# Paced loads, DMA transposes from block 10, and masks, inverse RMS and sink keys given to GpSimd, in an attention and SwGLU kernel

## The chip, the cores and the metric

One core of a Trainium2 chip. The metric is the device time of one execution, in microseconds. The kernel before takes 254.73 us (median of 3 runs, 254.19 to 254.93). A kernel that is only looked at gets a few runs; one that is compared closely gets 3 or 5 rounds next to the kernel before on the same chip.

Engines, as the profile abbreviates them: PE is TensorE (matmuls), PEld its weight loads, DVE VectorE, ACT ScalarE, POOL GpSimd, SP SyncE (here it only issues DMAs).

## The reference, cut to what matters

Attention with 4 sink keys and a window of 128, over 4 sequences of 768 tokens with 8 heads of 64, followed by RMSNorm and a SwGLU layer (512 to 1536 to 512):

```python
keep   = is_sink | in_window
scores = np.where(keep, q @ k.T / sqrt(D), -1e9)
a      = softmax(scores);  x = a @ v                     # (3072, 512)

rms  = np.sqrt(np.mean(x * x, axis=-1, keepdims=True) + 1e-06)
xn   = x / rms * rms_g
g    = xn @ w_gate
silu = g * (1.0 / (1.0 + np.exp(-g)))
out  = (silu * (xn @ w_val)) @ w_out
```

## The kernel before

Tokens go through in 24 blocks of 128, six to a sequence. For each block: load q, k, v; transpose q and k; scores, exp, mask; `a @ v` in two halves (`pv`), each normalised on VectorE to `x`; square and row sum on ScalarE (`sq`, `ms`); inverse square root in six operations of 128 x 1 (`m`, then five `y`); the scaled row `xr`; its transpose `xnt`. Four blocks make one group for the SwGLU layer: `pg` and `pvl` are the gate and value matmuls, `th` the tanh on ScalarE, `p` and `hT` two VectorE operations, `po` the matmuls with `w_out`. TensorE's program order is fixed by hand: attention of later blocks is woven into the SwGLU matmuls of an earlier group. What the change and the argument touch (`...` marks cuts):

```python
DMA_T_FROM = 12; POOL_MASK_FROM = 2
MANUAL = {PE, SP}                       # engines whose order is fixed by hand (names shortened)
ld = ctx.enter_context(tc.tile_pool(name="ld", bufs=3 * NT))   # 18 buffers for each of q and k
...
with tc.issue_after(last_load):         # everything from block 8 on, queued at once
    for g in range(2 * GB, NB):
        load_q(g); load_k(g); load_v(g)             # DMAs issued by GpSimd
...
def by_dma(g):
    return g >= DMA_T_FROM and g % NT > 0           # not the first block of a sequence
def unit_t(g):
    ...
    if by_dma(g):
        for i, src in enumerate((QS.pop(g), KS_.pop(g))):
            nc.sync.dma_start_transpose(out=QKT[b][:, i, :, t * P:(t + 1) * P], ...)
        return
    ps = ...; transposes(ps, ...); transposes(ps, ...); nc.scalar.copy(...)   # PE, then ACT
def unit_sink(b):
    ks = sink.tile([P, HP * KSW], BF16, name="ksk")
    nc.vector.memset(ks, 0.0)
    ... 2 x nc.vector.tensor_copy(out=ksv[...], in_=QKT[b][pr, 1, :, 0:NS])
def mask(ev, b, t, nq):
    if b < POOL_MASK_FROM or t == 0:
        nc.vector.tensor_tensor(out=e, in0=e, in1=mv, op=ALU.mult); return
    nc.gpsimd.affine_select(...)                    # one, or two of 128x512
...
def unit_av(g, u):
    ...                                             # pv matmuls
    unit_norm(g, u, pvv)                            # DVE: rden, x
    unit_sq(g, u)                                   # ACT: sq, ms
    if u == 1: unit_rms(g)                          # DVE: m, five y, then xr
def unit_rms(g):
    nc.vector.scalar_tensor_tensor(out=m, in0=ms[:, 0:1], scalar=RMS_EPS, in1=ms[:, 1:2], ...)
    nc.vector.tensor_scalar(out=y[:, 0:1].bitcast(I32), in0=m.bitcast(I32), ...)
    ... four more nc.vector.scalar_tensor_tensor, 128 x 1
    unit_xr(g)
def unit_xr(g):
    nc.vector.scalar_tensor_tensor(out=XR[g][-1], in0=x16[:, c], scalar=y[:, 4:5], in1=gb[:, c], ...)
```

The softmax here doesn't subtract the row's maximum and nothing guards it: scores larger than these inputs give would overflow.

## Time and profile before

| | before |
|---|---|
| median of 3 runs | 254.73 us |
| profiled span | 252.6 us |
| PE busy | 238.8 us (95%), so 13.8 us idle |
| granted PE clock | full throughout |
| DVE busy, POOL busy | 181.1 us, 98.1 us |

The page of the kernel before: the span, each engine's busy time with its share and its count of instructions, then rows of 40 slices of 6.3 us. A digit is the busy share of a slice in tenths; in the row PEclk it is the granted clock.

```profile
span 252.6 us, 4804 instructions
PE 238.8 (95%) x1733; PEld 127.4 (50%) x1760; DVE 181.1 (72%) x474; ACT 139.6 (55%) x312; POOL 98.1 (39%) x129
...
PE   5988979989999999999999999999999999999994
...
DVE  5666869889779999539989459988359991287700
...
POOL 8996779289985763134041004044201000000000
PEclk9999999999999999999999999999999999999999
```

From the tenth slice on the PE row is all nines up to the tail: a kernel that TensorE bounds. VectorE is also at nine in many slices and yet does not stop TensorE. (A row of nines means 90% or more; the clock here is full.)

### The profile page before, as it was taken

To read this page: it belongs to the slowest core of one execution; us is meant where nothing else is said; L and a number is where in the kernel's file an instruction comes from. 1 tells how busy PE (TensorE), PEld (TensorE's weight loads), DVE (VectorE), ACT (ScalarE), POOL (GpSimd) and SP (SyncE) were. 2 spreads that over 40 slices of the span, in tenths; PEclk is the share of its full clock that TensorE was granted. 3 is DMA by queue.
4 is the path that set the end of the run, shared out by engine and by line. 5 is a ranking of instruction groups with operands and counts; after the bars stand their busy time and mean duration, and the time that the engine had idled before them with its cause. 6 is when DMAs were issued, how large, how long until landed. Compare 5 with 4: busy or idle time off the path is not lost.

```text
span 252.6 us, 4804 instructions
## 1 busy us (share of the span) xinstructions
PE 238.8 (95%) x1733; PEld 127.4 (50%) x1760; DVE 181.1 (72%) x474; ACT 139.6 (55%) x312; POOL 98.1 (39%) x129
## 2 busy tenths in 40 slices
PE   5988979989999999999999999999999999999994
PEld 1446858655555454454454454454454544444441
DVE  5666869889779999539989459988359991287700
ACT  2757858879886465556473546466545441323211
POOL 8996779289985763134041004044201000000000
PEclk9999999999999999999999999999999999999999
DMA  9999999999999999650120550321321013200022
GB/s 130 152 174 189 189 156 188 182 155 150 194 186 161 155 131 155 128 168 13 21 56 10 145 145 3 64 58 19 113 84 23 0 21 98 91 0 0 0 86 83
DMA packets 105850, 25.74 MB, mean 102 GB/s; under 512 B 95074, under 2 KB 102754, under 8 KB 105827
## 3 DMA queue, kind: packets, MB, share of 16 engines
q0 software_dynamic: 80704, 13.90, 76.5%
q1 hardware_dynamic: 24082, 11.28, 18.6%
q10 hardware_dynamic: 1040, 0.26, 0.5%
q8 instruction: 14, 0.23, 0.4%
q14 instruction: 10, 0.07, 0.1%
HBM read 28.31 MB, written 6.29 MB: 137 GB/s over the span
## 4 chain that ended last, share of the span: by engine, by line
PE 67%; DMA 12%; DVE 8%; POOL 7%; ACT 2%; issue 2%; POOLq 0%; ACTq 0%; DVEq 0%
PE po L622 23%; PE pvl L581 18%; PE pg L581 18%; DMA wv<-in_moe_w_val_dram 7%; DMA ks<-in_k_dram 5%; PE pT L413 3%; DVE p L599 2%; POOL v L124 2%; POOL qs L111 2%; DVE hT L607 2%; PE pv L456 1%; PE pv L452 1%; PE pv L444 1%; POOL ks L111 1%; ACT et L422 1%
## 5 line engine op out<-in xcount | busy, mean ns | idle before, releaser
L581 PE MATMUL pg<-xnt,wg 128*128 128x512 bf16 (+1 forms) x317 | 73.5, 352 | 1.1 <-ACT xnt L567 0.5
L581 PE MATMUL pvl<-xnt,wv 128*128 128x512 bf16 (+1 forms) x322 | 73.4, 353 | 0.4
L622 PE MATMUL po<-wo,hT 128*128 128x512 bf16 x279 | 64.9, 379 | 0.5 <-issue 0.2
L594 ACT ACTIVATE th<-pg 128x512 bf16<-128x512 f32 x72 | 42.9, 596 | 39.1 <-PE pg L581 39.0
L599 DVE SCALAR_TENSOR_TENSOR p<-th,pg 128x512 bf16<-128x512 bf16 x72 | 48.9, 679 | 20.1 <-ACT th L594 19.5
L607 DVE TENSOR_TENSOR hT<-p,pvl 128x512 bf16<-128x512 bf16 x72 | 49.2, 684 | 3.7 <-PE pg L581 0.5
L581 PEld LDWEIGHTS <-wv 128*128 128x128 bf16 x328 | 30.5, 98 | 27.2 <-issue 1.1
L581 PEld LDWEIGHTS <-wg 128*128 128x128 bf16 x328 | 30.4, 98 | 26.9 <-issue 1.2
L422 ACT ACTIVATE et<-pT 128x512 bf16<-128x512 f32 x76 | 39.8, 602 | 4.8 <-PE pT L413 4.6
L390 POOL TENSOR_SCALAR_AFFINE_SELECT et<-et 128x512 bf16<-128x512 bf16 x20 | 13.1, 660 | 73.9 <-ACT et L422 73.9
L622 PEld LDWEIGHTS <-hT 128*128 128x128 bf16 x288 | 26.7, 98 | 29.7 <-issue 0.8
L494 ACT ACTIVATE sq<-x 128x256 bf16<-128x256 bf16 x48 | 20.0, 417 | 26.5 <-DVE x L484 26.1
L629 ACT ACTIVATE osb<-po 128x512 f32<-128x512 f32 x24 | 14.4, 602 | 25.9 <-PE po L622 20.8
L111 POOL DMA_DIRECT2D qs<-in_q_dram x23 | 20.7, 900 | 7.9 <-DMA wo<-in_moe_w_out_dram 2.2
L124 POOL DMA_DIRECT2D v<-in_v_dram x24 | 21.7, 903 | 4.4 <-DMA qs<-in_q_dram 2.6
L111 POOL DMA_DIRECT2D ks<-in_k_dram x23 | 20.6, 895 | 6.4 <-DMA wo<-in_moe_w_out_dram 3.2
L484 DVE TENSOR_TENSOR x<-pv,rden 128x256 bf16<-128x256 f32 x48 | 20.2, 421 | 0.8
L541 DVE SCALAR_TENSOR_TENSOR xr<-x,y,gb 128x512 bf16<-128x512 bf16 (+1 forms) x25 | 19.8, 795 | 0.7
L479 DVE RECIPROCAL rden<-pv 128x4 f32<-128x4 f32 x48 | 8.4, 175 | 16.1 <-PE pv L456 16.0
L388 DVE TENSOR_TENSOR et<-et,masks 128x1024 bf16<-128x1024 bf16 (+1 forms) x22 | 13.9, 638 | 3.5 <-ACT et L422 3.5
L456 PE MATMUL pv<-v,et 128*128 128x65 bf16 x168 | 15.3, 193 | 0.0
L452 PE MATMUL pv<-v,et 128*128 128x65 bf16 x136 | 12.7, 193 | 0.0
(75 smaller groups left out, 213.1 us busy)
## 6 DMA issues: line engine op xcount, KB each, us to landing
out_dram<-osb SPq DMA_DIRECT2D x24, 256.0 KB, 2.2
v<-in_v_dram POOLq DMA_DIRECT2D x24, 128.0 KB, 7.9
qs<-in_q_dram POOLq DMA_DIRECT2D x23, 128.0 KB, 8.2
ks<-in_k_dram POOLq DMA_DIRECT2D x23, 128.0 KB, 7.7
wg<-in_moe_w_gate_dram POOLq DMA_DIRECT2D x6, 256.0 KB, 7.6
wv<-in_moe_w_val_dram POOLq DMA_DIRECT2D x6, 256.0 KB, 8.2
wo<-in_moe_w_out_dram POOLq DMA_DIRECT2D x2, 768.0 KB, 10.6
osb<-in_k_dram ACTq DMA_DIRECT2D x1, 256.0 KB, 4.8
```

What stands on the lines that cost most here:

```text
L111: nc.gpsimd.dma_start(out=tl, in_=src[b, :, t * P:(t + 1) * P, :].rearrange("h t d -> t h d"),)
L124: nc.gpsimd.dma_start(out=V16[b][:, t, :, 0:D], in_=v[b, :, t * P:(t + 1) * P, :].rearrange("h t d -> t h d"),)
L422: nc.scalar.activation(out=et[:, hi].rearrange("p j n c -> p (j n c)"), in_=banks[u][hi], func=ACT.Exp, scale=inv_sqrt_d,)
L456: nc.tensor.matmul(out=dest, lhsT=E[(g, h, 0)], rhs=V16[b][:, t, h, :], start=(t == 0), stop=True, skip_group_check=True,)
L484: nc.vector.tensor_tensor(out=X16[g][:, heads_of(g, u), :], in0=pvv[:, :, 0:D], in1=RDEN.pop((g, u)).unsqueeze(2).to_broadcast((P, 4, D)), ...
L494: nc.scalar.activation(out=sq, in_=xh, func=ACT.Square, scale=MS_SCALE, accum_out=MS[g][:, u:u + 1],)
L541: nc.vector.scalar_tensor_tensor(out=XR[g][-1], in0=x16[:, c], scalar=y[:, 4:5], in1=gb[:, c], op0=ALU.mult, op1=ALU.mult,)
L581: nc.tensor.matmul(out=ps[:, i * n:(i + 1) * n], lhsT=w_sb[:, kt, ft * P:(ft + 1) * P], rhs=XNT[G][:, kt, cols], start=(kt == 0), stop=(kt ...
L594: nc.scalar.activation(out=st["th"], in_=st["pg"], func=ACT.Tanh, scale=0.5)
L599: nc.vector.scalar_tensor_tensor(out=p1, in0=st["th"], scalar=1.0, in1=st["pg"], op0=ALU.add, op1=ALU.mult,)
L607: nc.vector.tensor_tensor(out=HT[key][:, i:i + n, cols], in0=p1.rearrange("p (n c) -> p n c", n=n), in1=pvl.rearrange("p (n c) -> p n c", ...
L622: nc.tensor.matmul(out=st["po"], lhsT=HT[(G, ft // 2)][:, ft % 2, tb * P:(tb + 1) * P], rhs=wo[:, ft, :], start=(ft == 0), stop=(ft == FTN ...
```

## The change

Its intent: take load off TensorE (blocks 10, 11, 12 and 18 transposed by DMA) and off VectorE (six tiny operations of each block from 6, the masks of sequence 1 and the sink keys of sequences 1 to 3 to GpSimd), and issue the loads six blocks ahead instead of all at once, so that GpSimd, whose order is now fixed by hand too, comes to its other work. The diff, cut to its core:

```diff
-    DMA_T_FROM = 12
+    DMA_T_FROM = 10
+    LD = 4
+    AHEAD = 6
-    POOL_MASK_FROM = 2
-    MANUAL = {mybir.EngineType.PE, mybir.EngineType.SP}
+    POOL_MASK_FROM = 1
+    POOL_RMS_FROM = 6
+    MANUAL = {mybir.EngineType.PE, mybir.EngineType.SP, mybir.EngineType.Pool}
-    ld = ctx.enter_context(tc.tile_pool(name="ld", bufs=3 * NT))
+    ld = ctx.enter_context(tc.tile_pool(name="ld", bufs=LD))
-    with tc.issue_after(last_load):
-        for g in range(2 * GB, NB):
-            load_q(g); load_k(g); load_v(g)
+    def unit_load(g):
+        load_q(g); load_k(g); load_v(g)
     def by_dma(g):
-        return g >= DMA_T_FROM and g % NT > 0
+        return g >= DMA_T_FROM
     def unit_sink(b):
-        nc.vector.memset(ks, 0.0)
+        eng = nc.vector if b == 0 else nc.gpsimd
+        eng.memset(ks, 0.0)                      # the two copies likewise
     def unit_rms(g):
+        eng = nc.vector if g < POOL_RMS_FROM else nc.gpsimd
+        def fma(out, a, s1, op, s2, op1=ALU.mult):
+            eng.tensor_scalar(out=out, in0=a, scalar1=s1, scalar2=s2, op0=op, op1=op1)
-        ... one tensor_scalar and five scalar_tensor_tensor on nc.vector
+        fma(m, ms[:, 0:1], RMS_EPS, ALU.add, ms[:, 1:2], ALU.add)
+        ... five more fma: the same sums, as tensor_scalar with two scalar operands
     # in step(g):
+        if g + AHEAD < NB:
+            slots[2].append(lambda: unit_load(g + AHEAD))
```

More of the change, by code (lines that the diff above doesn't have):

```diff
@@ L238 @@
         load_wo(0)
-        last_load = load_wo(1)
-    with tc.issue_after(last_load):
-        for g in range(2 * GB, NB):
-            load_q(g)
-            load_k(g)
-            load_v(g)
+        load_wo(1)
     QKT, KSK, VSK, ESK, E, X16, MS, XR, XNT = {}, {}, {}, {}, {}, {}, {}, {}, {}
@@ L267, in unit_t1 @@
         )
+    def unit_load(g):
+        load_q(g)
+        load_k(g)
+        load_v(g)
     def by_dma(g):
-        return g >= DMA_T_FROM and g % NT > 0
+        return g >= DMA_T_FROM
     def unit_t(g):
@@ L296, in unit_sink @@
             pr = slice(hi * D, (hi + 1) * D)
-            nc.vector.tensor_copy(
+            eng.tensor_copy(
                 out=ksv[pr, :, hi * NS:(hi + 1) * NS],
@@ L469, in unit_av @@
             unit_rms(g)
-    PV, RDEN = {}, {}
+    PV, RDEN, LAST = {}, {}, [None]
     def heads_of(g, u):
@@ L483, in unit_norm @@
             unit_recip(g, u, pvv)
-        nc.vector.tensor_tensor(
+        LAST[0] = nc.vector.tensor_tensor(
             out=X16[g][:, heads_of(g, u), :], in0=pvv[:, :, 0:D],
             in1=RDEN.pop((g, u)).unsqueeze(2).to_broadcast((P, 4, D)), op=ALU.mult,
-        )
+        ).ins
     def unit_sq(g, u):
@@ L502, in unit_rms @@
         m = small.tile([P, 1], FP32, name="m")
-        nc.vector.scalar_tensor_tensor(
-            out=m, in0=ms[:, 0:1], scalar=RMS_EPS, in1=ms[:, 1:2],
-            op0=ALU.add, op1=ALU.add,
-        )
         y = small.tile([P, 5], FP32, name="y")
-        nc.vector.tensor_scalar(
-            out=y[:, 0:1].bitcast(I32), in0=m.bitcast(I32), scalar1=-0.5,
-            scalar2=float(0x5f3759df - 2 ** 31), op0=ALU.mult, op1=ALU.add,
-        )
-        nc.vector.scalar_tensor_tensor(
-            out=y[:, 1:2], in0=y[:, 0:1], scalar=y[:, 0:1], in1=m,
-            op0=ALU.mult, op1=ALU.mult,
-        )
-        nc.vector.scalar_tensor_tensor(
-            out=y[:, 2:3], in0=y[:, 1:2], scalar=RSQRT_B, in1=y[:, 1:2],
-            op0=ALU.add, op1=ALU.mult,
-        )
-        nc.vector.scalar_tensor_tensor(
-            out=y[:, 3:4], in0=y[:, 1:2], scalar=RSQRT_A, in1=y[:, 0:1],
-            op0=ALU.subtract, op1=ALU.mult,
-        )
-        nc.vector.scalar_tensor_tensor(
-            out=y[:, 4:5], in0=y[:, 2:3], scalar=RSQRT_C, in1=y[:, 3:4],
-            op0=ALU.add, op1=ALU.mult,
-        )
+        def fma(out, a, s1, op, s2, op1=ALU.mult):
+            eng.tensor_scalar(out=out, in0=a, scalar1=s1, scalar2=s2, op0=op, op1=op1)
+        fma(m, ms[:, 0:1], RMS_EPS, ALU.add, ms[:, 1:2], ALU.add)
+        fma(y[:, 0:1].bitcast(I32), m.bitcast(I32), -0.5, ALU.mult,
+            float(0x5f3759df - 2 ** 31), ALU.add)
+        fma(y[:, 1:2], y[:, 0:1], y[:, 0:1], ALU.mult, m)
+        fma(y[:, 2:3], y[:, 1:2], RSQRT_B, ALU.add, y[:, 1:2])
+        fma(y[:, 3:4], y[:, 1:2], RSQRT_A, ALU.subtract, y[:, 0:1])
+        fma(y[:, 4:5], y[:, 2:3], RSQRT_C, ALU.add, y[:, 3:4])
         Y[g] = y
@@ L734 @@
         ], first=True)
-        slots = [[lambda: unit_t1(5, 0)], [lambda: unit_t1(5, 1)], [lambda: unit_s(4)], [lambda: unit_sink_scores(0, 4)], [lambda: unit_t(6)], []]
+        slots = [[lambda: unit_t1(5, 0)], [lambda: unit_t1(5, 1), lambda: unit_load(8)], [lambda: unit_s(4)], [lambda: unit_sink_scores(0, 4), lambda: unit_load(9)], [lambda: unit_t(6)], [lambda: unit_load(10)]]
         for g in range(5, NB + 3):
```

## The prediction

> **What bounds it now.** TensorE. The busy table gives PE 95%, and the matmuls also run at rate: four 128x512 matmuls take 0.86 us wherever they stand in a row (chain of waits). Counting the columns of all matmuls at that rate, about 236 of the 252.6 us are streaming. By ten-us stretches, the 60 to 249 us part is about full; the idle is at the start (3.2 us in 0-10), in loads (1.3, 1.0, 1.6 us in 10-40, 1.4 us in 50-60, of which 1.2 us waits for q and k of block 8 behind w_out), and 3.7 us of tail. DMA is 90% or more busy for the first 105 us, but after 60 us PE no longer waits for it. DVE is 94-98% busy in several stretches (80-100, 150-170, 190-210) and stands in the chain there, yet PE hardly loses time.
>
> **What changes, costed.**
> 1. Blocks 10, 11, 12 and 18 are transposed by DMA: 4 x 0.44 us of PE (eight 128-column transposes) and 4 ACT copies of 1.01 us go. PE gain: 1.7 us, the only sure one.
> 2. DVE loses six tiny operations of each block from 6 (about 1.15 us a block, 20 us in all), the masks of blocks 7-11 (8 x 0.69 and 2 x 0.42 us) and most sink-key work. It was not what limited PE, so this buys little.
> 3. POOL gains this and must now run in program order: per block 3 load issues (0.88 us each = 2.6), masks 4 x 0.6 = 2.4, inverse RMS as six mostly dependent operations (estimate 0.26 us each, from two dependent 128x8 selects that started 0.26 us apart: 1.5 us). That is 6.5 us a block, while blocks 7-10 pass through PE in 5.3 to 6 us.
> 4. The loads from block 8 are paced. The first 50 us of DMA keep their order, so the wait for block 8 stays.
>
> **Where it hurts.** With four load buffers, POOL's load of block 12 waits for the DMA transposes of block 10, whose k lands near 57 us (issue 49.95 + 7.0). Transposes landed 7-8 us after issue under the full queue, 2.4 us when free; so that load is issued near 59-61, and behind it in order stand the masks of block 7 and the sink keys of sequence 1. PE wanted them at 60.9 and 60.4 (sink scores); I expect them near 64-66. POOL then has work without a break to about 85 us and lags again for the masks of block 8 and the inverse RMS of blocks 6 and 7, whose xr the PE transposes need. PE stalls of 5-7 us in 60-85. Later, DVE's fixed order holds xr right behind the norm, so it waits for square, then POOL: 1-2 us a block, giving back what it saved, with up to 1-3 us lost where the w_out matmuls wait for the last hT.
>
> The Trainium skill (GPSIMD Engine Reference, Key points) says POOL shares SBUF interfaces with VectorE; this trace agrees: one y operation took 0.60 us at 154.6 beside POOL's mask and 0.15 us at 164.6 without.
>
> **Sum.** 254.7 - 1.7 + about 7 = 260 us. Range 254 to 267. Faster by 2% would need 5 us, more than the removed PE work can give.
>
> **What would show it.** PE streaming down 1.7 us; PE idle in 60-85 waiting on POOL (masks, ksk) and xr; POOL busy without gaps there; DVE busy down by 20 us or more but idle before xr on POOL; DMA no longer full after 60 us; q and k transposes near 2.4 us later on.
>
> **What would make it wrong.** POOL tiny operations much quicker than 0.26 us, block 10's transposes landing by 58, or loads issued faster: then about 253. Slower tiny operations (0.4 us): 270.

## More of the kernel before

The waits of the kernel before: engine and line, what it waited for, total us, times, longest.

```profile
POOL et L390 <- ACT et L422: 73.9, 10, 17.4
...
DVE p L599 <- ACT th L594: 19.5, 22, 9.6
```

GpSimd idles before its masks, which costs nothing. VectorE waits for ScalarE (the second line) and TensorE; no wait for GpSimd is among its larger ones.

What matters later is the place where a group's SwGLU matmuls end and its `w_out` matmuls begin. The timeline of the kernel before at the last of these: start, duration, engine, line, operation, output and inputs, count.

```profile
207.22 0.22 DVE L513 SCALAR_TENSOR_TENSOR y<-y,m 128x1 f32<-128x1 f32 x1
207.28 5.99 PE L622 MATMUL po<-wo,hT 128*128 128x512 bf16 x27
207.36 0.68 DVE L599 SCALAR_TENSOR_TENSOR p<-th,pg 128x512 bf16<-128x512 bf16 x1
...
208.14 0.69 DVE L607 TENSOR_TENSOR hT<-p,pvl 128x512 bf16<-128x512 bf16 x1
208.75 0.15 DVE L525 SCALAR_TENSOR_TENSOR y<-y 128x1 f32<-128x1 f32 x1
208.94 0.75 DVE L541 SCALAR_TENSOR_TENSOR xr<-x,y,gb 128x512 bf16<-128x512 bf16 x1
```

The tiny operations and the last `p` and `hT` interleave on one engine: the hT that the twelfth `po` matmul needs is done at 208.83, and TensorE goes on without a gap.

## The result, and the profile after

The kernel after is correct and takes **280.44 us** (median of 4 runs, 279.60 to 282.22) against 254.83 us of the kernel before on the same chip (4 runs). The ratio is 1.102, interval 1.096 to 1.108. Here and below a ratio is the mean time of one kernel's fast runs over that of the other's in the same rounds, so it is not quite the ratio of the medians quoted.

The page of the kernel after (40 slices of 7.0 us):

```profile
span 278.6 us, 4823 instructions
PE 247.1 (89%) x1702; PEld 129.3 (46%) x1728; DVE 161.5 (58%) x347; ACT 134.4 (48%) x308; POOL 144.8 (52%) x264
...
PE   6978979984968989699999799998899995999994
...
DVE  4656867891332787725768446977247683067710
...
POOL 8987684619999755597766721565344202000000
PEclk9979989997799999999999999999999997999999
```

TensorE has 32 matmuls fewer to do (count the weight loads: 1760 and 1728), yet its idle time rises from 13.8 to 31.5 us (span less busy), and its busy time rises too, by 8.3 us, because slices of the PEclk row now read 7 or 8: matmuls ran at a lower clock. VectorE is relieved of 19.6 us and idles. GpSimd is at nine for four slices in a row (63 to 91 us).

The waits of the kernel after:

```profile
DVE xr L531 <- POOL y L510: 47.3, 18, 9.1
...
POOL m L510 <- ACT sq L497: 28.1, 7, 8.5
...
PE po L612 <- DVE hT L597: 8.5, 4, 3.5
...
POOL qs L113 <- DMA qkT<-ks: 7.0, 2, 6.5
...
PE pss L324 <- POOL ksk L300: 3.4, 1, 3.4
```

The first line is the new wait: VectorE stands before `xr` until GpSimd has the inverse RMS, at each of 18 blocks, 2.6 us on average. The third is what TensorE pays for it at the ends of the groups, exactly four times. The second is GpSimd's own wait for the row sums; the last two are a second story.

**The first place, 54 to 75 us.** GpSimd's timeline in the kernel after (the square bracket is the idle time before, and what ended it):

```profile
61.91 0.88 POOL L113 DMA_DIRECT2D qs<-in_q_dram  x1 [6.55 <-DMA qkT<-ks]
...
67.50 0.43 POOL L300 COPY ksk<-qkT 64x16 bf16<-64x16 bf16 x2
...
70.62 0.31 POOL L510 TENSOR_SCALAR m<-ms 128x1 f32<-128x1 f32 x1
71.02 0.19 POOL L510 TENSOR_SCALAR y<-m 128x1 int32<-128x1 int32 x1
71.31 0.34 POOL L510 TENSOR_SCALAR y<-y,m 128x1 f32<-128x1 f32 x1
71.75 0.92 POOL L510 TENSOR_SCALAR y<-y 128x1 f32<-128x1 f32 x3
72.62 0.64 POOL L393 TENSOR_SCALAR_AFFINE_SELECT et<-et 128x512 bf16<-128x512 bf16 x1
73.22 1.08 POOL L398 TENSOR_SCALAR_AFFINE_SELECT et<-et 128x512 bf16<-128x512 bf16 x1
...
78.25 0.30 POOL L510 TENSOR_SCALAR m<-ms 128x1 f32<-128x1 f32 x1
```

With four buffers, block 12's load of q stood still for 6.55 us, until the DMA transpose of block 10's k had landed (issued at 58.93, landed 2.8 us later; in e1 and h4 too the load starts within 0.2 us of that landing). Why it was block 10's transpose that freed the buffer, and not block 8's, isn't shown; that the number of buffers makes the wait, e2 shows. Everything behind it in program order (masks of block 7, sink keys, inverse RMS of block 6) is late. From there each block takes 7.6 us of GpSimd (70.62 to 78.25). TensorE and VectorE at the same time, in two timelines of the kernel after:

```profile
67.99 1.03 PE L324 MATMUL pss<-qkT,ksk 128*128 128x256 bf16 x4 [3.42 <-POOL ksk L300]
...
69.27 3.60 PE L612 MATMUL po<-wo,hT 128*128 128x512 bf16 x8
...
76.18 1.89 PE L612 MATMUL po<-wo,hT 128*128 128x512 bf16 x8
```

```profile
72.71 1.10 DVE L531 SCALAR_TENSOR_TENSOR xr<-x,y,gb 128x512 bf16<-128x512 bf16 x1 [9.12 <-POOL y L510]
```

Eight `po` matmuls took 3.60 us after the wait of 3.42 us, and 1.89 us later on. The kernel after in four stretches there: bounds, length, then busy time and count of PE, PEld, DVE, ACT and POOL, granted clock, DMA share (which can exceed 1 in this view), GB/s.

```profile
64.50:68.00 3.50, 0.08 (x2) 0.02 (x2) 0.00 (x0) 1.66 (x4) 3.40 (x9) 0.77 1.59 167
68.00:71.40 3.40, 3.40 (x18) 1.77 (x19) 0.00 (x0) 0.39 (x1) 3.12 (x6) 0.50 1.19 119
71.40:74.80 3.40, 3.32 (x25) 1.62 (x25) 2.02 (x5) 0.35 (x2) 3.21 (x7) 0.73 1.05 67
74.80:78.00 3.20, 3.20 (x26) 1.77 (x27) 0.10 (x1) 3.16 (x10) 3.20 (x5) 1.00 0.35 81
```

TensorE idle, then busy at clock 0.50, then full again. The clock was at half for 6.8 us in all (1.6, 3.4 and 1.8 us by the shares of the first three stretches), from about 66.4 to 73.2 us. The Trainium skill (TensorE: Matmul & The Clock Gate, Part 1: The HAM clock gate) says that the array drops to half rate after one idle window of about 3.4 us and returns after about 3.4 us of sustained work. This trace agrees in the unit, 6.8 us being two such windows, but not in the moments: the half clock began 1.8 us after TensorE had stopped (64.57) and ended 5.2 us after it had started again (67.99).

**The second place, the end of each group's SwGLU matmuls.** The timeline of the kernel after at the last of them, to be held against the one of before:

```profile
229.99 0.30 POOL L510 TENSOR_SCALAR m<-ms 128x1 f32<-128x1 f32 x1 [7.42 <-DVE hT L597]
...
232.06 0.75 DVE L531 SCALAR_TENSOR_TENSOR xr<-x,y,gb 128x512 bf16<-128x512 bf16 x1 [2.11 <-POOL y L510]
232.72 0.68 DVE L589 SCALAR_TENSOR_TENSOR p<-th,pg 128x512 bf16<-128x512 bf16 x1
233.51 0.69 DVE L597 TENSOR_TENSOR hT<-p,pvl 128x512 bf16<-128x512 bf16 x1
...
234.25 6.95 PE L612 MATMUL po<-wo,hT 128*128 128x512 bf16 x24 [3.46 <-DVE hT L597]
```

The tanh that `p` needs was ready at 230.38 (229.80 + 0.58 on ScalarE, in the same timeline), but `p` is queued behind `xr`, and `xr` waits for GpSimd until 232.06. TensorE has used up the eleven `po` matmuls that it could do and stands for 3.46 us; its clock then reads 0.83 over 230 to 240 us.

**The sum.** Span +26.0 us = idle +17.7, busy +8.3; with 1.7 us of work removed, the busy time is stretched by about 10. The clock alone (mean 0.968 over 278.6 us) accounts for up to 8.9 us of that, so the rest, about 1 us, is not placed. The 8.9 us are an upper bound: the run of this kernel with a mean clock of 0.982 took 280.58 us, no less than the two with 0.968 (280.30 and 279.60). The first 60 us lost no more idle time than before (8.3 and 8.5 us) but had 6.8 us at half clock; 3.4 us of that, in 10 to 20 us, is chance, as the experiments show; the other 3.4 us, in 39 to 43 us, are in e1 and e3 too and not in h4, and their cause is open.

### The profile page after: what moved, and what is told of

Same layout as the page of the kernel before. It is cut to its first block, busy times and chain, and to the rows that moved or that the text cites. A ratio compares the mean times of both kernels' runs of the same rounds, so it can differ in the third digit from the quotient of the medians.

```text
span 278.6 us, 4823 instructions
## 1 busy us (share of the span) xinstructions
PE 247.1 (89%) x1702; PEld 129.3 (46%) x1728; DVE 161.5 (58%) x347; ACT 134.4 (48%) x308; POOL 144.8 (52%) x264
## 4 chain that ended last, share of the span: by engine, by line
PE 32%; DVE 25%; POOL 24%; issue 9%; ACT 5%; DMA 3%; POOLq 0%; DVEq 0%; ACTq 0%
PE po L612 11%; PE pg L571 9%; DVE p L589 8%; PE pvl L571 8%; POOL y L510 8%; DVE hT L597 7%; DVE xr L531 5%; POOL et L398 3%; POOL v L126 3%; DMA ks<-in_k_dram 3%; POOL et L393 2%; POOL qs L113 2%; DVE x L487 2%; POOL ks L113 2%; POOL m L510 2%
## 5 line engine op out<-in xcount | busy, mean ns | idle before, releaser
L571 PE MATMUL pg<-xnt,wg 128*128 128x512 bf16 (+1 forms) x321 | 74.5, 356 | 2.9 <-ACT xnt L557 1.2
L612 PE MATMUL po<-wo,hT 128*128 128x512 bf16 x279 | 68.4, 392 | 9.0 <-DVE hT L597 8.5
L584 ACT ACTIVATE th<-pg 128x512 bf16<-128x512 f32 x72 | 42.0, 595 | 31.9 <-PE pg L571 31.3
L531 DVE SCALAR_TENSOR_TENSOR xr<-x,y,gb 128x512 bf16<-128x512 bf16 (+1 forms) x25 | 23.0, 923 | 47.4 <-POOL y L510 47.3
L510 POOL TENSOR_SCALAR m<-ms 128x1 f32<-128x1 f32 x18 | 5.4, 301 | 59.7 <-ACT sq L497 28.1
L113 POOL DMA_DIRECT2D qs<-in_q_dram x23 | 21.5, 934 | 13.0 <-DMA qkT<-ks 7.0
L393 POOL TENSOR_SCALAR_AFFINE_SELECT et<-et 128x512 bf16<-128x512 bf16 x30 | 20.4, 684 | 0.0
L398 POOL TENSOR_SCALAR_AFFINE_SELECT et<-et 128x512 bf16<-128x512 bf16 x24 | 20.2, 841 | 0.0
L510 POOL TENSOR_SCALAR y<-y 128x1 f32<-128x1 f32 x54 | 14.7, 281 | 3.5
```

What stands on the lines that cost most here:

```text
L113: nc.gpsimd.dma_start(out=tl, in_=src[b, :, t * P:(t + 1) * P, :].rearrange("h t d -> t h d"),)
L393: nc.gpsimd.affine_select(out=ev[:, :, 0, :], in_=ev[:, :, 0, :], compare_op=ALU.is_ge, fill=0.0, base=0, pattern=[[0, x], [1, P]], channe ...
L398: nc.gpsimd.affine_select(out=ev[:, :, 1, :], in_=ev[:, :, 1, :], compare_op=ALU.is_ge, fill=0.0, base=-1, pattern=[[0, x], [-1, P]], chan ...
L510: eng.tensor_scalar(out=out, in0=a, scalar1=s1, scalar2=s2, op0=op, op1=op1)
L571: nc.tensor.matmul(out=ps[:, i * n:(i + 1) * n], lhsT=w_sb[:, kt, ft * P:(ft + 1) * P], rhs=XNT[G][:, kt, cols], start=(kt == 0), stop=(kt ...
L584: nc.scalar.activation(out=st["th"], in_=st["pg"], func=ACT.Tanh, scale=0.5)
```

## The experiments

Two theories, and the letters some expectations use:

- **H, the hand-off.** The inverse RMS on GpSimd costs the time, because `xr` stands in VectorE's fixed order right behind the norm, so that `p` and `hT` wait behind it for ScalarE, then GpSimd. (VectorE's order isn't set by hand here but when the program is built; it is fixed once the kernel runs.)
- **Q, the queue of loads.** The four load buffers make GpSimd wait at block 12, and the lateness passes on; the hand-off is only its carrier.
- A third suspicion, for the part that neither explains: masks and sink keys are too much for GpSimd, or the two-scalar form of the tiny operations is dearer, or the DMA transposes are late.

All were run in three calls, with the kernel before at 254.85, 255.16 and 254.79 us. Overview:

| run | us (median) | ratio to before |
|---|---|---|
| after | 280.44 | 1.102 |
| e1: inverse RMS on VectorE | 261.84 | 1.027 |
| e2: 18 load buffers | 275.07 | 1.078 |
| f1: both | 254.42 | 1.000 |
| g1: `xr` queued later | 267.02 | 1.046 |
| g2: `xr` later, 18 buffers | 260.30 | 1.021 |
| e3: masks and sink keys on VectorE | 284.34 | 1.115 |
| h4: masks alone on VectorE | 275.63 | 1.085 |
| e4: before, all transposes from block 10 by DMA | 266.47 | 1.042 |
| h2: before, only blocks 10 and 11 more | 257.17 | 1.005 |
| e5: before, two-scalar form | 257.10 | 1.008 |
| h1: f1 with the old form | 254.15 | 0.998 |
| h3: GpSimd only from block 8, late `xr` | 256.29 | 1.007 |

All give the correct result. The medians are of all runs and the ratios of fast runs alone; g1 has one slow run far off (below), e4 and h4 have one of four and h2 two of six over 1.5% above their own fastest, which count as slow. The medians of their fast runs are 266.63 (g1), 266.10 (e4), 275.42 (h4) and 255.83 us (h2); the differences below are taken from these.

### e1: the inverse RMS back on VectorE

```diff
-    POOL_RMS_FROM = 6
+    POOL_RMS_FROM = 99
```

> The changed kernel with one part undone: the inverse RMS of blocks 6 to 23 back on VectorE. Theory H (hand-off): most of the 25.6 us come from the round trip square on ScalarE, six operations of 2.0 us on GpSimd, then xr, behind which VectorE's fixed order stands still (47.3 us of waiting of xr for GpSimd in the trace). Then this gives 256 to 261 us: the 1.7 us of TensorE saved, but the wait of the sink scores of sequence 1 for GpSimd (3.4 us, and the half clock after it) stays. Theory Q (queue): GpSimd is overloaded and blocked by the paced loads whatever it does; taking 2 of some 8 us a block from it leaves over half of the loss, 268 us or more. Theory C (the clock alone): no change beyond 2 us, 278 or more.

Measured 261.84 us (261.35 to 262.44), ratio 1.0266 (1.0216 to 1.0316). The four waits of `po` for hT are gone; what is left on TensorE is the first place. GpSimd waits there for the load's buffers as before (6.49 us, to 62.18). One line of TensorE's timeline in this run:

```profile
68.24 1.03 PE L324 MATMUL pss<-qkT,ksk 128*128 128x256 bf16 x4 [5.05 <-POOL ksk L300]
```

It is a little above the upper end of what H gave, and far below what Q asked for. The hand-off is worth 18.6 us (280.44 less 261.84), the larger part; not all. What is left, 7.4 us over f1 below, goes with this one wait of 5.05 us: the rest can be the half clock after it (6.8 us in this trace).

### e2: eighteen load buffers

```diff
-    LD = 4
+    LD = 3 * NT
```

> The changed kernel with 18 load buffers instead of 4, nothing else: GpSimd's load of block 12 then needn't wait for the DMA transposes of block 10 (6.55 us of GpSimd idle at 55 to 62 us). Theory Q: this wait is what starts the loss; 268 us or less. Theory H: only the wait of the sink scores at 64.6 to 68 and the half clock after it (together some 5 us) go; 273 to 277 us. In both the wait of 3.4 us before the sink scores is gone.

Measured 275.07 us (274.10 to 275.65), ratio 1.0781. The load no longer waits for the transposes, and 5.4 us come back. VectorE still waits 43.6 us for the inverse RMS and TensorE 8.3 us for hT. So Q is real and the smaller part. From the waits of this run:

```profile
DVE xr L531 <- POOL y L510: 43.6, 18, 5.9
```

### f1: both

The edits of e1 and e2 together.

> The changed kernel with the two undone that moved the time down: inverse RMS on VectorE and 18 load buffers (e1 and e2 together). If the two causes (hand-off of the inverse RMS; the load of block 12 waiting for the transposes of block 10, ahead of sink keys and masks) are the whole loss: 253 to 257 us, beside 261.8 with the first alone, and no TensorE wait for the sink keys. If masks and sink keys on GpSimd, or the paced loads themselves, cost something of their own: 259 us or more.

Measured 254.42 us (254.38 to 256.53), ratio 1.0002 (0.9964 to 1.0040). Nothing of the loss is left. Its page:

```profile
span 252.6 us, 4773 instructions
PE 238.7 (95%) x1702; PEld 126.5 (50%) x1728; DVE 176.6 (70%) x455; ACT 135.7 (54%) x308; POOL 111.1 (44%) x156
...
PEclk9999999999999999999999999999999999999999
```

The two causes together are the whole loss. They are not quite a sum: undone alone they give back 18.6 and 5.4 us, 24.0, and undone together 26.0 (280.44 less 254.42), so each costs a little more beside the other. With all the rest of the change in place (paced loads, sequence 1's masks and the sink keys on GpSimd, the two-scalar form, the DMA transposes) the kernel is as fast as before, to 0.4% either way. It is not faster, although TensorE has 32 transposes fewer.

### g1: the same work on GpSimd, `xr` queued later

H says that it is VectorE's order that hurts, not the slowness of GpSimd. So the chain stays on GpSimd, and only `xr` moves in VectorE's order, behind the first norm of the next block:

```diff
-        if g >= 2:
+        if 2 <= g < XR_LATE_FROM:                       # XR_LATE_FROM = 6
             unit_xr(g)
+    def xr_late(g):
+        with tc.issue_after(LAST[0]):
+            unit_xr(g)
     # in step(g):
+        if XR_LATE_FROM <= g - 2 < NB:
+            slots[1].append(lambda: xr_late(g - 2))
```

> The changed kernel with only xr moved in VectorE's order: it stands behind the first norm of the next block instead of right behind its own block's second norm. GpSimd does exactly the same work in the same order. Theory H (VectorE stands still in its fixed order through the round trip, and hT behind it is late for the w_out matmuls): most of the waits of xr for GpSimd (47 us) and nearly all TensorE waits of w_out matmuls for hT (8.5 us) go; 264 to 271 us. Theory Q (GpSimd has too much to do): VectorE's order changes nothing, 277 us or more.

Measured 266.63 us in its three fast runs (266.12 to 267.42; ratio 1.0457, 1.0428 to 1.0486); the fourth, the profiled one, took 291.88 us in the slow state, so its lines are not used. 13.8 of the 18.6 us come back (280.44 less 266.63) without moving a single operation off GpSimd.

### g2: g1 with eighteen buffers

> g1 with 18 load buffers as well. If hand-off order and load blocking are the two causes and add up: 5 us below g1, 258 to 266 us, with the inverse RMS still on GpSimd. If GpSimd's amount of work is itself the limit: no better than 270.

Measured 260.30 us (260.14 to 261.16), ratio 1.0212. The waits of this run, taken to stand for g1's as well:

```profile
DVE xr L532 <- POOL y L511: 10.5, 4, 4.2
...
PE pxt L554 <- DVE xr L532: 7.4, 5, 2.5
```

VectorE's wait falls from 43.6 us (e2) to 10.5. What remains over f1 is 5.9 us: the blocks 6 and 7, whose `xr` TensorE itself transposes, come too late for it (7.4 us of waiting, against 3.1 in f1, then 3.4 us at half clock in 70 to 80 us), and one `po` waits 1.3 us at 215. This part I put down to the length of GpSimd's chain; no run shortens it.

Moving `xr` did one thing more. In the kernel after, the end of the chain starts `xr` and GpSimd's next operation at the same moment: the 14 of the 18 `xr` of blocks 6 to 23 that begin beside GpSimd's masks take 1.09 or 1.10 us, the four that don't 0.75. In g2 four of the 18 take over 1 us. How much of the 13.8 us is this, and how much the order, isn't separated.

### e3: masks of sequence 1 and all sink keys on VectorE

```diff
-    POOL_MASK_FROM = 1
+    POOL_MASK_FROM = 2
-        eng = nc.vector if b == 0 else nc.gpsimd
+        eng = nc.vector
```

> The changed kernel with the masks of sequence 1 and the sink keys of sequences 1 to 3 back on VectorE; the inverse RMS stays on GpSimd. Theory H: the hand-off is untouched, 274 us or more. Theory Q: GpSimd has 2.4 us a block less to do from block 7 to 11 and the sink keys no longer stand behind blocked loads; 268 us or less.

Measured 284.34 us (283.53 to 285.86), ratio 1.1154: slower than the kernel after. Taking work off the overloaded GpSimd made it worse, which I had not expected. In its waits VectorE stood 9.8 us, in two pieces, before the sink-key copies for the DMA transposes of blocks 12 and 18. The next two runs say why.

### e4: the kernel before, with the transposes of blocks 10, 11, 12 and 18 by DMA

```diff
-    DMA_T_FROM = 12
+    DMA_T_FROM = 10
-        return g >= DMA_T_FROM and g % NT > 0
+        return g >= DMA_T_FROM
```

> The kernel before with the DMA transposes of the change alone (blocks 10, 11, 12, 18 added), loads as before. If only TensorE's removed time counts: 253 us (1.7 us less). If the transposes of blocks 10 to 12, which land 7 to 8 us after issue while the loads fill the DMA queues, come late for the scores of blocks 10 and 11: 1 to 4 us more than that, 254 to 257 us, with a TensorE wait on a qkT transpose near 70 to 80 us.

Measured 266.47 us (264.16 to 268.48; fast runs 266.10), ratio 1.0416. Both expectations were wrong by some ten microseconds. VectorE's timeline of this run:

```profile
77.07 0.35 DVE L297 COPY ksk<-qkT 64x16 bf16<-64x16 bf16 x2 [8.00 <-DMA qkT<-ks]
```

The sink keys are the first four keys of a sequence's first block. When that block is transposed by TensorE they come early. By DMA, under the full queue of loads that the kernel before keeps, the transposes of block 12 took about 8.4 us to land, and VectorE stood in front of its copy for 8.00 us (3.9 more at block 18). TensorE's largest waits were then 4.0, 2.6 (in two pieces) and 2.5 us, and it ran 6.8 us at half clock. So moving the sink keys to GpSimd looks like the part of the change that made this transposing bearable: on VectorE the copy is a hand-off too, from a DMA. h4 against e3, below, tests it.

### h2: the kernel before, with only blocks 10 and 11 more

```diff
-    DMA_T_FROM = 12
+    DMA_T_FROM = 10
```

> The kernel before with blocks 10 and 11 (not the first blocks of a sequence, 12 and 18) transposed by DMA too. If e4's 11.6 us came from VectorE's sink-key copies waiting for the DMA transposes of blocks 12 and 18 (8.0 and 3.9 us), they are gone: 253.5 to 255.5 us. If transposes of blocks 10 and 11 landing 8 us late under the early loads were a part of it: 257 us or more.

Measured 257.17 us over all six runs (254.43 to 259.29) and 255.83 in the four fast ones, ratio 1.0052 (1.0006 to 1.0098): between the two expectations, with a wide spread. The profiled run, at 258.19 us the slowest of the fast ones, has one TensorE wait of 3.2 us for block 11's transposed q, so late transposes have a part too. Without first blocks of a sequence most of e4's loss is gone (266.10 to 255.83), which ties it to the transposes of blocks 12 and 18; a gain is not there either.

### h4: the kernel after, with the masks alone on VectorE

```diff
-    POOL_MASK_FROM = 1
+    POOL_MASK_FROM = 2
```

> The changed kernel with only the masks of sequence 1 back on VectorE (sink keys stay on GpSimd). e3 was slower than the changed kernel, but in it VectorE's sink-key copies waited 9.8 us for DMA transposes. If that wait was the reason: this is 272 to 279 us, a little better than 280.4, since GpSimd has 2.4 us a block less in blocks 7 to 11. If masks on VectorE themselves cost: 281 us or more.

Measured 275.63 us (273.66 to 277.85; fast runs 275.42), ratio 1.0849: 5.0 us better than after. So in e3 the masks helped and the sink keys cost, about 8.9 us (284.34 less 275.42). The GpSimd masks of sequence 1 are a part of the loss in the kernel after; in f1, where they are on GpSimd too, no loss is left.

### e5: the kernel before, with the two-scalar form of the tiny operations, all on VectorE

The edit is the body of `unit_rms` from the change with `eng = nc.vector`.

> The kernel before with the inverse RMS written as in the change (six two-scalar operations) but all on VectorE; nothing else. The three operations with a pointer in the place of the second tensor took 0.27 instead of 0.22 us and 0.21 instead of 0.15 in the first 20 us of the two traces, 0.23 us more a block. If this form is what lost the changed kernel 2.6 us in its first 20 us (xr later, TensorE idle and then at half clock): 256 us or more. If that loss is chance of the clock at the start: within 1 us of before.

Measured 257.10 us (256.70 to 257.54, 5 rounds), ratio 1.0080 (1.0061 to 1.0099). The groups of the same two operations, first in this run, then in the kernel before: busy us, mean ns of one, idle before.

```profile
L508 DVE TENSOR_SCALAR y<-y,m 128x1 f32<-128x1 f32 x24 | 6.5, 273 | 0.8
L508 DVE TENSOR_SCALAR m<-ms 128x1 f32<-128x1 f32 x24 | 5.1, 211 | 4.1 <-ACT sq L495 4.1
```

```profile
L513 DVE SCALAR_TENSOR_TENSOR y<-y,m 128x1 f32<-128x1 f32 x24 | 5.4, 224 | 0.7
...
L503 DVE SCALAR_TENSOR_TENSOR m<-ms 128x1 f32<-128x1 f32 x24 | 3.8, 159 | 4.4 <-ACT sq L494 4.3
```

The same sum costs 50 ns more as `tensor_scalar` with two [128, 1] operands than as `scalar_tensor_tensor`. Here that was worth 2.0 us in all.

### h1: f1 with the old form

The edits of f1, and the six operations as in the kernel before.

> f1 with the inverse RMS in its old three-operand form: of the change there stay the DMA transposes of blocks 10, 11, 12, 18, the paced loads (18 buffers), masks of sequence 1 and sink keys on GpSimd. e5 showed the two-scalar form to cost 2.0 us, so if the causes add up: 252 to 253 us, 0.7 to 1.1% below before, which is the 1.7 us of TensorE work taken away. If f1 hides another loss or gain: outside 251 to 254.

Measured 254.15 us (253.64 to 255.22, 5 rounds), ratio 0.9984 (0.9958 to 1.0010). I had expected 252 to 253, adding e5's 2.0 us to f1. From f1 to h1 it was 0.3 us, so the 2.0 us do not add. The best version is this one, and it is not shown to be faster than the kernel before. The profile has 12.2 us of idle TensorE, against 13.8 before, and no lowered clock up to the last 2 us; where the 1.7 us of removed transposes went is not settled.

### h3: the hand-off only where DMA transposes `xr`, queued late, with the old form before

g2 with the chain on GpSimd only from block 8, and `xr` late from 8.

```diff
-    POOL_RMS_FROM = 6
-    XR_LATE_FROM = 6
+    POOL_RMS_FROM = 8
+    XR_LATE_FROM = 8
```

> g2 with the inverse RMS on GpSimd only from block 8 (whose xr goes to TensorE by DMA, not by TensorE transposes that wait for it) and the old form on VectorE before that. In g2 the TensorE transposes of blocks 6 and 7 waited over 4 us more for xr than in f1, and TensorE then ran 3.4 us at half clock. Theory H: with slack at both ends the hand-off costs nothing but a wait of 1.3 us of the last block: 252 to 255 us. If GpSimd's work still slows others (shared ports): 257 us or more. In no theory is it below h1 by over 1 us, since VectorE was not what TensorE waited for.

Measured 256.29 us (255.99 to 258.46), ratio 1.0072, above what I expected. With blocks 6 and 7 on VectorE, 4 of g2's 5.9 us come back (260.30 less 256.29; the form of the operations differs as well). Even with all that is known here, the inverse RMS on GpSimd gains nothing.

### Half clock that comes and goes

In 10 to 20 us the profiles of after, e1, e3, g2, h2 and h3 have 3.4 us at half clock, and those of before, e2, e4, f1, e5, h1 and h4 none. h2 and the kernel before run the same program there. So half clock in that place is chance, and is not put down to the change. It also costs little: among the runs of the kernel before in the second call, four with a clock of 0.992 or 0.993 took 255.4 us on average and four with 0.999 or 1.000, the warmest, 254.9 (in the first and third call the same two groups are 1.4 and 0.2 us apart). Some of the matmuls there are dummies, whose result nobody reads (11 of them from 10 to 16 us in the kernel before).

Nor does a wait's length alone decide. In g2 a wait of 2.5 us (to 75.42) was followed by 3.4 us at half clock; in h2 one of 3.2 us was not, and in h4 one of 3.4 us, before `po` at a group's end as in the kernel after, was not either. A stretch of h4 that holds it, with the columns of the table above (clock 1.00, and 1.00 in the ten us after it too):

```profile
220.00:230.00 10.00, 6.58 (x34) 2.81 (x31) 5.62 (x11) 3.07 (x8) 1.63 (x6) 1.00 0.07 13
```

## Why the prediction was wrong, point by point

**Right.** TensorE bound the kernel. The 32 matmuls, estimated at 1.7 us, are gone, though no run shows them as a gain in time (h1: 0.9984, up to 1.0010). The direction was right, and so was the first place, with its mechanism: block 12's load blocked behind block 10's transposes (predicted issue 59 to 61, measured 61.91), masks and sink keys late (predicted 64 to 66; masks 64.5 to 66.9, sink scores at 67.99), GpSimd without gaps to about 85 us (measured about 93), stalls of 5 to 7 us of TensorE in 60 to 85 (measured 6.3 us idle there, 0.2 before). VectorE's busy time fell by 19.6 us (predicted 20 or more) and bought nothing.

**Wrong: the last term.** "Later, DVE's fixed order holds xr right behind the norm, so it waits for square, then POOL: 1-2 us a block, giving back what it saved, with up to 1-3 us lost where the w_out matmuls wait for the last hT." The mechanism is the one that e1, g1 and g2 show; this term was mis-sized. The wait was 2.6 us a block (47.3 over 18). At the group ends TensorE waited 8.5 us in four waits (idle in the four ten-us stretches that hold them: 9.2 us, against 0.3 us before), and 3.4 us at half clock followed the last. I counted the wait against the VectorE time it freed. But VectorE's free time is worth nothing to TensorE, and the wait stands directly in front of `p` and `hT`, which TensorE needs at once when a group ends and no other matmul is in its order. All of the hand-off, the first place included, cost 18.6 us, of which 13.8 go with the place of `xr` in VectorE's order. Of the 20 us by which the sum of 260 fell short, the group ends are 6 to 8 (8.9 us of added idle against 1 to 3) and the half clock, which no term held, up to 8.9.

**Wrong: the chain's length.** Predicted 1.5 us at 0.26 us an operation, from two selects; measured 2.00 us (70.62 to 72.62), 0.29 to 0.44 us from start to start where single operations can be told apart. I take start to start because the Trainium skill (Perfetto Trace Analysis, GPSIMD Engine Instruction) calls a GpSimd instruction's reported span unreliable; here the spans, 0.19 to 0.34 us, are indeed shorter than the spacing. The prediction did name this: "Slower tiny operations (0.4 us): 270". GpSimd's step is 7.6 us a block instead of 6.5: 2.0 for the chain (1.5), 2.8 for the masks (2.4), 2.8 for the loads (2.6).

**Missing: the clock.** Nothing in the prediction says that a TensorE wait of some 3 us can also slow the matmuls after it. The mean clock of 0.968 is worth up to 8.9 us of span. The Trainium skill (TensorE: Matmul & The Clock Gate, Why this matters for your kernels) warns of just this, gaps of over about 3 us between matmuls, and I did not use it. Here the waits of 3.42 and 3.46 us in the kernel after and of 5.05 us in e1 were followed by half clock, the 3.2 us of h2 and the 3.4 us of h4 were not. A predicted stall of 5 to 7 us in one place should have been booked with half-clock time.

**Missing: how hand-offs trade.** I took the sink-key move as mere load on GpSimd. e4 and e3 show that it belongs to the DMA transposes: left on VectorE it costs 8 us of waiting for a transpose (e4), and 8.9 us of the whole (e3 against h4).

**Contention, right in kind.** The shared interfaces that the prediction takes from the Trainium skill (GPSIMD Engine Reference, Key points) can be seen again: the `xr` at 72.71 took 1.10 us while GpSimd masked (a mask beside it 1.08), the one at 232.06 took 0.75 us with GpSimd idle. The hand-off makes such meetings the rule, 14 of 18; at 0.35 us each that is 4.9 us of VectorE, small next to 47.3 us of waiting.

**"DMA no longer full after 60 us" was half right.** The DMA share fell to 0.96 in 60 to 70 us (2.52 before), but the loads were spread over the kernel (the last is issued at 158 us; the share is 1.21 in 160 to 170), where before the share was 0.22 from 110 to 120.

## What to carry to other kernels

A tiny operation moved to an idle engine is not free because that engine is idle: its result has to come back, and on an engine that keeps its order, as VectorE did here, everything queued behind the consumer waits for it. Before you move it, look at what stands behind the consumer and who needs that next; queueing the consumer later was worth 13.8 us here with the same work on the same engines; moving the work back, 18.6. Free time won on an engine that isn't the bottleneck is no credit against waits, and a TensorE wait of about 3 us should be booked at more than its length, for the half clock that can follow it.

## What the Trainium skill lacked or had wrong

- GPSIMD Engine Reference (section 3.1) costs elementwise work of 512 and 2048 elements, and in its table of costs gives a dispatch figure only for VectorE. A chain of 128 x 1 operations has none: here 0.29 to 0.44 us from start to start on GpSimd, 2.00 us for six.
- TensorE: Matmul & The Clock Gate gives windows of 3.4 us, and the half clock here came in pieces of 3.4 or 6.8 us. But its rule, no gaps over about 3 us, did not part the waits that half clock followed (2.5 us in g2, 3.42 and 3.46 in the kernel after, 5.05 in e1) from those that it did not (3.2 us in h2, 3.4 in h4); and h2 had 3.4 us at half clock in 10 to 20 us with 1.2 us of idle there in all, h4 none with 1.6 us. The page says that the window runs freely, which may be why; no run here tests it.
- DMA: Bandwidth & Descriptors says which engines issue transposes, but has nothing on how long one takes to land behind a full queue of loads: for the transposes of q and k 2.4 us when free, 7.1 us at most in the kernel after, 8.7 us in e4 and 9.3 us for the late q of h2.
- No page found compares `tensor_scalar` with two [128, 1] operands with `scalar_tensor_tensor` for the same sum: 0.211 and 0.159 us for `m`, 0.273 and 0.224 us for `y * y * m`, and 2.0 us of the whole in e5.
